# Second half of a linear-attention and MLP block: the attention product by seven products, the last two products by column block, the last stores on two queues

## The chip, the cores and the metric

The kernel runs on one core of one Trainium2 chip. The metric is the device time of one execution in microseconds, the median of the runs. The engines are TensorE (PE, with its weight loads listed as PEld), VectorE (DVE), ScalarE (ACT), GpSimd (POOL) and SyncE (SP, which here only issues DMAs).

## The reference

Input x is 2048 tokens of 512 features, all in float32. It is normalised, and two blocks are added to it: a linear attention with 32 heads and a two-layer MLP with a squared relu.

```python
xn = layernorm(x)
# A: q, k, v = xn @ wqkv, by head (H = 32, Dh = 16); phi(t) = (t + 1 if t > 0 else exp(t)) + 1e-6
kv = einsum("bhsd,bhse->bhde", phi(k), v)
z = phi(k) summed over s
o = (phi(q) @ kv) / (phi(q) . z + 1e-6)
A = o.reshape(B, S, D) @ wo
# B: F = 1376
r = max(xn @ w1 + b1, 0)
B = (r * r) @ w2 + b2
out = x + A + B
```

## The kernel before

**Precision.** Every float32 operand of a product is split into a high part and a rest (`split`: a copy on ACT into the reduced type, then a subtraction on DVE), and a product is three matmuls: high by high, rest by high, high by rest. Splits of weights ("ops") are written once to scratch in DRAM (`wd1`, `wd2`, `wdz`) and loaded back when needed; splits of activations ("s") are made just ahead of use by `parts_of` into one of five rotating tiles (`pair`).

**Stages.** The first stage takes the 16 tiles of 128 tokens one by one: normalise, transpose, keys, and the sum of phi(k) by x. From that sum the kernel forms kv and then `M = kv @ wo` per head, in four blocks of 128 rows which are written to DRAM (`wdm`). From there on the attention output is one product with `M`, whose rows stand beside those of `w2`. The second stage runs twice (`for n in range(2)`), each time over two blocks of 512 tokens, t1 and t2.

**One pass of the second stage.** A loop over `p` makes the hidden rows in pairs of 128-row tiles: `NQ = 2` pairs of queries (k = 0, 1) and `NP = 5` pairs of the MLP (k = 2 to 6), `NK = 7` in all. A pair of two tiles by two token blocks is a 2x2 block product, and `product` does it by seven block products instead of eight, with sums of weights made by `make_1` and sums of tokens `T[1]` to `T[4]`. The four results of pair k are `h[k, 0]` to `h[k, 3]` (relu and square for the MLP, phi and division for the queries).

The results are then multiplied by the rows of `w2` and `M`. In the first pass (n = 0) that is done directly, eight block products for each pair. In the second pass (n = 1) the MLP pairs go by seven products as well: `combinations(k)` makes sums of the four tiles on DVE, `make_t` made the matching sums of `w2` during the first pass (on DVE and ACT into the tiles `made`, which lie in the places `rp0` and `rp1`, and from there by a DMA to `wd2`). The tiles `rp0` and `rp1` are used again by the hidden tiles of the last pair (k = 6) of the second pass. Products 0 and 1 of an MLP pair are done inside the loop (`add_product`), products 4, 5, 3, 6, 7 behind it, in phases of one product over all five pairs (`phase_jobs`), which share two banks of PSUM named X, Y, Z, W and V. The attention pairs are done directly in this pass, by two groups of `attentions` (four tiles each, both halves of the columns), and each group ends with the odd eleventh row tile of the MLP (`z_job`, tile `hz`).

The order of jobs in the second pass is: Y by product 4, then attention and z on Z and Y, X by 5, Y by 3, X by 6, attention and z on V and W, V by 7. Between them, `copies` saves banks through ACT (`m1`, `m5`, `u2`), `add_to` adds on DVE, `turned_to` transposes on DVE and adds to the residual tile `res`, and `store` writes it out: eight DMAs of 128 KB for a block of 512 tokens, four for each half of the columns.

**Order.** All operations behind the first tiles are recorded and not issued at once. `Program.order` plays them through with estimated costs (`cost`) 60 times and issues them in the best order it found; PE's order is as recorded, that of the other engines is free within the dependencies. `nc.emit` issues all of them from one line, L295, so the profile tells them apart by tiles. A DMA is issued by SP, in its queue's order. Operands lie in eight places of 512 KB (`D0` to `D7`), filled in the order in which `needed_in` lists them as places come free.

`second` multiplies one pair of operand tiles by one split tile, six matmuls for two column blocks c, alternating between them; with `end` the last call does three for one block and then three for the other.

Of the kernel before, what the change touches and what calls it, by code (L numbers as in the profile page):

```python
# [12 lines left out]

P = 128
H = 32
REORDER = True


# [55 lines left out]
class Program:  # L74
# [60 lines left out]
    def cost(self, t, out, ins):  # L135
        n = 1
        for s, k in list(out.ap)[1:]:
            n *= k
        src = n
        for a in ins:  # L140
            m = 1
            for _, k in list(a.ap)[1:]:
                m *= k
            src = max(src, m)
        t.lock, t.size, t.lag = False, 0, 0.06
        if t.engine == "tensor":
            wide = t.name == "matmul" and ins[0].dtype != F32
            t.dur, t.lag = (0.0135 + n / 2400 if wide else 0.055 + n / 2400 if t.name == "transpose" else 0.11 + n / 1200), 0.23
        elif t.engine == "scalar":
            ps = any(map(in_psum, ins))  # L150
            t.dur = (0.2 if ps else 0.22) + src / 1250 + (0.09 if t.kw.get("bias") is not None and n > 64 and not isinstance(t.kw.get("bias"), float) else 0)
        elif t.engine == "vector":
            a, b = self.DVE.get(t.name, (0.1, 0.5))
            t.dur = a + src * b / 960
            t.lock = t.name in ("tensor_tensor", "scalar_tensor_tensor") and n > 64 and not any(map(in_psum, ins))
        elif t.engine == "gpsimd":
            t.dur = 0.2 + src * 2.3 / 1000 if t.name == "tensor_tensor" else 0.3
            t.lock = t.name == "tensor_tensor"
# [16 lines left out]
    def order(self):  # L175


        ts = self.tasks
        for t in ts:
            t.succs = []  # L180
        for t in ts:
            for place in t.first:
                for o in place.tasks:
                    t.preds.setdefault(o.index, 1)
            t.left = len(t.preds)
        for t in ts:
            for p, raw in t.preds.items():
                ts[p].succs.append((t, raw))
        line = [t for t in ts if not t.left]
        for t in line:  # L190
            for s, raw in t.succs:
                s.left -= 1
                if not s.left:
                    line.append(s)
        when = 0.0
        for t in ts:
            t.due = 1e9
            if t.engine == "tensor":
                t.due = when
                when += t.dur  # L200
        for t in reversed(line):
            e = t.engine
            took = t.dur if e != "sync" else t.lag + t.size / 320e3
# [29 lines left out]
    def play(self):  # L233
# [18 lines left out]
        while done < len(ts):  # L252
# [27 lines left out]
            if e == "sync":  # L280
                dma = end = max(dma, end) + t.size / 320e3
            done += 1
            for s, raw in t.succs:
                ready = end + (t.lag if e == "sync" or raw and s.engine != e else 0.0)
# [22 lines left out]
def kernel(  # L307
# [495 lines left out]
    def needed_in(n):  # L803
# [77 lines left out]

    ORDER = ((0, 0), (1, 0), (0, 1))

    def second(ps, key, s, first=False, last=False, end=False):

        a = op(*key)
        for n, (u, v), c in [(n, uv, c) for c in range(2) for n, uv in enumerate(ORDER)] if end else \
                [(n, uv, c) for n, uv in enumerate(ORDER) for c in range(2)]:
            nc.tensor.matmul(ps[c], lhsT=a[:, u * 256 + c * P:u * 256 + (c + 1) * P], rhs=s[:, v],
                             start=first and n == 0, stop=last and n == 2, skip_group_check=True)  # L890
        used()

    def second_z(ps, cs, s, first=False, last=False):
# [359 lines left out]
    for n in range(2):  # L1253
# [23 lines left out]
        def finish(k, i, src):  # L1277
# [9 lines left out]
            else:  # L1287
# [8 lines left out]
                elif n:  # L1296
                    square(o)

        def add_product(k, i):
            if n == 0:  # L1300
                for v in range(2):
                    second(acc[2 * v:2 * v + 2], ("2", k - NQ, 2 * i + v), s[k, i], k == NQ and i == 0)
            else:
                second(acc[2 * i:2 * i + 2], ("2", k - NQ, 2 * i), s[k, i], k == NQ)

        def combinations(k):

# [94 lines left out]
        if n == 0:  # L1402
# [14 lines left out]
            def step(e):  # L1417
# [6 lines left out]
                if e > 3:  # L1424
                    if not made_t and sorted(raw_free) == ["rp0", "rp1", "x0", "x1"]:
                        raw_free[:] = ["x0", "x1"]
                        raw_jobs.extend(raw_2(k, "t") for k in range(NP))
                        fetch_raws()
                    if len(raw_free) < 4:
                        for u in range(2 * (len(made_t) < NP)):  # L1430
# [21 lines left out]
            assert len(made_t) >= NP, made_t  # L1452
            do(outs, len(outs))
            do(columns, len(columns))
            do(sums, len(sums))
# [21 lines left out]
        def turned_to(t, a, src):  # L1477
            for c in range(2):
                add_turned(res[t], a + c, src[c])

        def strassen(ps, k, i, first=False, last=False):
            return lambda: h[k][i], lambda s: second(ps, ("2", k - NQ, i), s, first, last, i == 7 and last)

        def phase_jobs(ps, i, first=False, last=False):
            return [strassen(ps, k, i, first and k == NQ, last and k == NK - 1) for k in pairs_f]

        def attentions(ps, e, first, last):
            return [(lambda j=j: h[j // 2, e + j % 2], attention_job(ps, e, j, first and j == 0)[1]) for j in range(NJ)] +                    [(lambda: hz[:, e // 2], z_job(ps, e, last)[1])]
# [8 lines left out]
        o = {}  # L1497
        at_end(lambda: o.update(m5=copies("m5", Y)))
        jobs += attentions([*Z, *Y], 0, False, False)
        at_end(lambda: (add_to(m1, Z), turned_to(t1, 0, m1)))  # L1500
        jobs += phase_jobs(X, 5)
        at_end(lambda: o.update(u2=copies("u2", X)))
        jobs += phase_jobs(Y, 3, False, True)
        at_end(lambda: (add_to(o["u2"], Y), turned_to(t1, 2, o["u2"]), store(res[t1], t1, 0, 1)))
        jobs += phase_jobs(X, 6, False, True)
        at_end(lambda: (add_to(o["m5"], X), turned_to(t2, 0, X)))
        jobs += attentions([*V, *W], 2, True, False)
        at_end(lambda: (add_to(o["m5"], W), turned_to(t2, 2, o["m5"]), store(res[t2], t2, 1)))
        jobs += phase_jobs(V, 7, False, True)
        at_end(lambda: (turned_to(t2, 0, V), store(res[t2], t2, 0)))  # L1510

        def prepare_s(job):
            return parts_of("s", job[0]()) if job[0] else None
# [32 lines left out]
```

## Time and profile before

| | |
|---|---|
| time, median of 3 runs | 415.73 us (415.72 to 415.8) |
| profiled execution | 415.67 us, span 414.0 us |
| PE busy | 404.5 us, 1808 instructions |
| DVE busy | 326.8 us |
| ACT busy | 256.4 us |
| POOL busy | 27.8 us |
| DMA | 96.19 MB, mean 232 GB/s |
| granted PE clock | 0.998 |

Span is the time from the first to the last event of the profiled execution; the execution's own time also holds what lies around it. Busy time counts each engine's instructions by themselves; a share of the span says little about a single stage. The chain of waits follows the last instruction back to what released it. A timeline row gives start, length, engine, operation, tiles (out<-in), the count and, in brackets, how long the engine was idle before it and who ended that.

### The profile page before, as it was taken

To read this page: it belongs to the slowest core of one execution; us is meant where nothing else is said; L and a number is where in the kernel's file an instruction comes from. 1 tells how busy PE (TensorE), PEld (TensorE's weight loads), DVE (VectorE), ACT (ScalarE), POOL (GpSimd) and SP (SyncE) were. 2 spreads that over 40 slices of the span, in tenths; PEclk is the share of its full clock that TensorE was granted. 3 is DMA by queue.
4 is the path that set the end of the run, shared out by engine and by line. 5 is a ranking of instruction groups with operands and counts; after the bars stand their busy time and mean duration, and the time that the engine had idled before them with its cause. 6 is when DMAs were issued, how large, how long until landed. Compare 5 with 4: busy or idle time off the path is not lost.

```text
span 414.0 us, 5503 instructions
## 1 busy us (share of the span) xinstructions
PE 404.5 (98%) x1808; PEld 334.2 (81%) x1808; DVE 326.8 (79%) x551; ACT 256.4 (62%) x438; POOL 27.8 (7%) x48
## 2 busy tenths in 40 slices
PE   8999999999999999999999999999999999999993
PEld 7788888888888888888888888888888887888882
DVE  6898998899788989999989350999999766376943
ACT  5786665666777998899943220477877677335310
POOL 2242322220000000000000000000000000000000
PEclk9999999999999999999999999999999999999999
DMA  7862636914979786963999997897866589958604
GB/s 239 283 185 76 160 114 149 290 53 156 359 245 364 225 290 243 329 225 156 357 320 269 357 375 297 236 289 276 275 220 192 194 236 260 287 178 252 181 0 102
DMA packets 78272, 96.19 MB, mean 232 GB/s; under 512 B 40002, under 2 KB 51266, under 8 KB 77988
## 3 DMA queue, kind: packets, MB, share of 16 engines
q1 hardware_dynamic: 78244, 95.84, 74.1%
q8 instruction: 14, 0.23, 0.2%
q14 instruction: 14, 0.11, 0.1%
HBM read 59.91 MB, written 33.82 MB: 226 GB/s over the span
## 4 chain that ended last, share of the span: by engine, by line
PE 96%; DVE 2%; DMA 1%; ACT 0%; issue 0%
PE ps L295 51%; PE acc L295 45%; DMA x<-in_A_x_dram 1%; DVE res L295 0%; DVE o L295 0%; DVE st L295 0%; DVE xp L295 0%; DVE y L295 0%; ACT rr L295 0%; DVE mv L295 0%
## 5 line engine op out<-in xcount | busy, mean ns | idle before, releaser
L295 PE MATMUL ps<-s,ops 128*128 128x512 f32 x390 | 92.9, 389 | 0.0
L295 PEld LDWEIGHTS ps<-s,ops 128*128 128x128 f32 x390 | 73.1, 188 | 15.3 <-ACT s L295 0.2
L295 PE MATMUL acc<-s,ops 128*128 128x512 f32 x300 | 72.7, 390 | 0.8 <-ACT rr L295 0.8
L295 PEld LDWEIGHTS acc<-s,ops 128*128 128x128 f32 x300 | 56.2, 188 | 13.1 <-ACT rr L295 1.2
L295 PE MATMUL acc<-pk,tok 128*128 128x512 f32 x192 | 47.0, 394 | 0.0
L295 DVE TENSOR_TENSOR s<-rr,s 128x512 fp32r<-128x512 f32 x46 | 31.6, 689 | 17.2 <-ACT s L295 16.2
L295 ACT ACTIVATE s<-rr 128x512 fp32r<-128x512 f32 x46 | 28.9, 631 | 24.4 <-PE acc L295 13.9
L295 PEld LDWEIGHTS acc<-pk,tok 128*128 128x128 f32 x192 | 35.5, 188 | 7.8 <-DVE pk L295 0.5
L295 PE MATMUL ps<-T,ops 128*128 128x512 f32 x168 | 41.4, 390 | 0.0
L295 PE MATMUL acc<-T,ops 128*128 128x512 f32 x168 | 41.2, 389 | 0.0
L295 PEld LDWEIGHTS acc<-T,ops 128*128 128x128 f32 x168 | 31.5, 188 | 6.6
L295 PEld LDWEIGHTS ps<-T,ops 128*128 128x128 f32 x168 | 31.5, 188 | 6.5
L295 POOL TENSOR_TENSOR tok<-xp,tok 128x512 fp32r<-128x512 f32 x16 | 22.9, 1432 | 42.1 <-ACT tok L295 35.1
L295 PE MATMUL ps<-xs0h,ops 128*128 128x512 f32 x72 | 23.6, 389 | 0.0
L295 ACT ACTIVATE rr<-acc 128x512 f32<-128x512 f32 x23 | 13.5, 588 | 15.0 <-PE acc L295 14.8
L295 DVE TENSOR_TENSOR ops<-raw,ops 128x512 fp32r<-128x512 f32 (+1 forms) x28 | 18.7, 676 | 1.5 <-ACT ops L295 1.3
L295 ACT ACTIVATE k<-ps 128x512 f32<-128x512 f32 x16 | 9.5, 595 | 15.7 <-PE ps L295 15.6
L295 ACT ACTIVATE ops<-raw 128x512 fp32r<-128x512 f32 (+1 forms) x28 | 16.3, 593 | 4.4 <-PE acc L295 2.4
L295 PE MATMUL acc<-xs0h,ops 128*128 128x512 f32 x56 | 18.4, 389 | 0.0
L295 ACT ACTIVATE s<-rf 128x512 fp32r<-128x512 f32 x10 | 6.3, 633 | 18.0 <-PE ps L295 17.6
L295 DVE TENSOR_TENSOR rr<-acc,rr 128x512 f32<-128x512 f32 x21 | 14.4, 684 | 3.8 <-PE acc L295 1.7
L295 ACT ACTIVATE rr<-rr,odds 128x512 f32<-128x512 f32 x15 | 10.8, 723 | 9.2 <-DVE rr L295 9.1
(152 smaller groups left out, 734.5 us busy)
## 6 DMA issues: line engine op xcount, KB each, us to landing
ops<-wd SPq DMA_DIRECT2D x43, 512.0 KB, 5.3
wd<-ops SPq DMA_DIRECT2D x35, 512.0 KB, 4.8
ops<-wd SPq DMA_DIRECT2D x42, 256.0 KB, 3.8
wd<-made SPq DMA_DIRECT2D x10, 512.0 KB, 5.7
res<-in_A_x_dram SPq DMA_DIRECT2D x32, 128.0 KB, 6.0
out_dram<-res SPq DMA_DIRECT2D x32, 128.0 KB, 3.7
x<-in_A_x_dram SPq DMA_DIRECT2D x5, 512.0 KB, 6.3
raw<-in_B_w_dram SPq DMA_DIRECT2D x10, 256.0 KB, 5.2
```

The lines of the kernel that those rows point to most:

```text
L295: getattr(getattr(self.nc, t.engine), t.name)(*map(real, t.args), **{k: real(a) for k, a in t.kw.items()})
```

## The change

In the second pass the attention pairs join the seven products. `make_t` now also makes combined weights for the two pairs of `M`, `combinations` is also run for k = 0 and 1, and the products 0 and 1 of these pairs become four direct jobs at the front of the job list, into the banks X and Z that `add_product` uses. The phases run over seven pairs, in the order 2, 3, 4, 5, 0, 1, 6. The groups `attentions` are gone; `second_z` stands alone where they were. The first phase comes after the direct jobs.

In the last phase (product 7 into V) the last two pairs, 1 and 6, are held back and done together: all six matmuls of column block 0, then all six of column block 1. Of the last four stores two are issued by ACT instead of SP. The planner's cost function is taught that ACT can issue a DMA.

```diff
+LAST = 2
...
-        elif t.engine == "scalar":
+        elif t.engine == "scalar" and t.name != "dma_start":
...
-        keys = [("2", f, 4) for f in range(NP)]
-        keys.insert(NP - 2, ("2", NP - 1, 2))
+        keys = [("2", f, i) for f in (NP, NP + 1) for i in (0, 2)]
+        keys.insert(3, ("2", NP - 1, 2))
...
+        order = (*range(NP - 1), NP, NP + 1, NP - 1)
+        keys += [("2", f, 4) for f in order]
         flush_keys()
-        attention(False)
         both_of("z", 0, 2)
-        keys += [("2", f, i) for i in (5, 3, 6) for f in range(NP)]
+        keys += [("2", f, i) for i in (5, 3, 6) for f in order]
         flush_keys()
-        attention(False)
         both_of("z", 0, 2)
-        keys += [("2", f, 7) for f in range(NP)]
+        keys += [("2", f, 7) for f in order]
...
-    def second(ps, key, s, first=False, last=False, end=False):
-
-        a = op(*key)
-        for n, (u, v), c in [(n, uv, c) for c in range(2) for n, uv in enumerate(ORDER)] if end else \
-                [(n, uv, c) for n, uv in enumerate(ORDER) for c in range(2)]:
+    def second(ps, key, s, first=False, last=False, before=None):
+
+        todo = [(op(*k), b) for k, b in (before or []) + [(key, s)]]
+        steps = [(n, uv, c, k) for n, uv in enumerate(ORDER) for c in range(2) for k in range(1)]
+        if before:
+            steps = [(n, uv, c, k) for c in range(2) for k in range(len(todo)) for n, uv in enumerate(ORDER)]
...
-    def store(r, t, *halves):
+    def store(r, t, *halves, by=None):
         for g, h, rows in out_blocks(of, t):
             if h in halves:
-                nc.sync.dma_start(rows, r[g, h])
+                (by or nc.sync if g.start % 64 else nc.sync).dma_start(rows, r[g, h])
...
-                        raw_jobs.extend(raw_2(k, "t") for k in range(NP))
+                        raw_jobs.extend(raw_2(k, "t") for k in range(NK))
...
-        pairs_f = range(NQ, NK)
+        pairs_f = (*range(NQ, NK - 1), *range(NQ), NK - 1)
...
+        def combined(k, i):
+            if k not in h:
+                run(*combinations(k))
+            return h[k][i]
...
-        m1 = copies("m1", X)
-        jobs, ends = phase_jobs(Y, 5 - 1, True), {}
...
-        jobs.insert(NP - 2, (None, lambda s: add_product(NK - 1, 1)))
+        jobs = [direct(k, i) for k in range(NQ) for i in range(2)]
+        ends[4] = [lambda: o.update(m1=copies("m1", X))]
+        jobs += phase_jobs(Y, 4, True)
+        jobs.insert(3, (None, lambda s: add_product(NK - 1, 1)))
         at_end(lambda: o.update(m5=copies("m5", Y)))
-        jobs += attentions([*Z, *Y], 0, False, False)
+        jobs.append((lambda: hz[:, 0], lambda s: second_z([*Z, *Y], range(NJ), s)))
...
-        jobs += attentions([*V, *W], 2, True, False)
+        jobs.append((lambda: hz[:, 1], lambda s: second_z([*V, *W], range(NJ), s, True)))
...
         jobs += phase_jobs(V, 7, False, True)
-        at_end(lambda: (turned_to(t2, 0, V), store(res[t2], t2, 0)))
+        at_end(lambda: (turned_to(t2, 0, V), store(res[t2], t2, 0, by=nc.scalar)))
```

More of the change, by code (lines that the diff above doesn't have):

```diff
@@ L202, in order @@
             e = t.engine
-            took = t.dur if e != "sync" else t.lag + t.size / 320e3
+            took = t.dur if not t.size else t.lag + t.size / 320e3
             for s, raw in t.succs:
@@ L279, in play @@
             last = max(last, end)
-            if e == "sync":
+            if t.size:
                 dma = end = max(dma, end) + t.size / 320e3
@@ L283, in play @@
             for s, raw in t.succs:
-                ready = end + (t.lag if e == "sync" or raw and s.engine != e else 0.0)
+                ready = end + (t.lag if t.size or raw and s.engine != e else 0.0)
                 if ready >= s.ready:
@@ L882 @@
     ORDER = ((0, 0), (1, 0), (0, 1))
-    def second(ps, key, s, first=False, last=False, end=False):
-        a = op(*key)
-        for n, (u, v), c in [(n, uv, c) for c in range(2) for n, uv in enumerate(ORDER)] if end else \
-                [(n, uv, c) for n, uv in enumerate(ORDER) for c in range(2)]:
-            nc.tensor.matmul(ps[c], lhsT=a[:, u * 256 + c * P:u * 256 + (c + 1) * P], rhs=s[:, v],
-                             start=first and n == 0, stop=last and n == 2, skip_group_check=True)
+    def second(ps, key, s, first=False, last=False, before=None):
[3 more added lines that the diff above has]
+            steps = [(n, uv, c, k) for c in range(2) for k in range(len(todo)) for n, uv in enumerate(ORDER)]
+        for n, (u, v), c, k in steps:
+            a, b = todo[k]
+            nc.tensor.matmul(ps[c], lhsT=a[:, u * 256 + c * P:u * 256 + (c + 1) * P], rhs=b[:, v],
+                             start=first and n == 0 and k == 0, stop=last and n == 2 and k == len(todo) - 1, skip_group_check=True)
         used()
@@ L1297, in finish, with row_of @@
                     square(o)
+        def row_of(k):
+            return k - NQ if k >= NQ else NP + k
         def add_product(k, i):
@@ L1303, in add_product @@
             else:
-                second(acc[2 * i:2 * i + 2], ("2", k - NQ, 2 * i), s[k, i], k == NQ)
+                second(acc[2 * i:2 * i + 2], ("2", row_of(k), 2 * i), s[k, i], k == NQ)
         def combinations(k):
@@ L1426, in step @@
                         raw_free[:] = ["x0", "x1"]
-                        raw_jobs.extend(raw_2(k, "t") for k in range(NP))
+                        raw_jobs.extend(raw_2(k, "t") for k in range(NK))
                         fetch_raws()
                     if len(raw_free) < 4:
-                        for u in range(2 * (len(made_t) < NP)):
+                        for u in range(2 * (len(made_t) < NK)):
                             make_t(len(made_t), u)(work.tile([P, 2, 512], F32R, name="made", tag=f"rp{u}"))
@@ L1451 @@
                      lambda j: prepare(j), 2, step)
-            assert len(made_t) >= NP, made_t
+            assert len(made_t) >= NK, made_t
             do(outs, len(outs))
@@ L1479, in turned_to, with direct @@
                 add_turned(res[t], a + c, src[c])
+        def combined(k, i):
+            if k not in h:
+                run(*combinations(k))
+            return h[k][i]
         def strassen(ps, k, i, first=False, last=False):
-            return lambda: h[k][i], lambda s: second(ps, ("2", k - NQ, i), s, first, last, i == 7 and last)
+            return lambda: combined(k, i), lambda s: later.append((("2", row_of(k), i), s)) if i == 7 and k in pairs_f[-LAST:-1] else                     second(ps, ("2", row_of(k), i), s, first, last, later if i == 7 and last else None)
         def phase_jobs(ps, i, first=False, last=False):
-            return [strassen(ps, k, i, first and k == NQ, last and k == NK - 1) for k in pairs_f]
-        def attentions(ps, e, first, last):
-            return [(lambda j=j: h[j // 2, e + j % 2], attention_job(ps, e, j, first and j == 0)[1]) for j in range(NJ)] +                    [(lambda: hz[:, e // 2], z_job(ps, e, last)[1])]
-        m1 = copies("m1", X)
-        jobs, ends = phase_jobs(Y, 5 - 1, True), {}
+            return [strassen(ps, k, i, first and k == pairs_f[0], last and k == pairs_f[-1]) for k in pairs_f]
+        def direct(k, i):
+            return lambda: h[k, i], lambda s: second(acc[2 * i:2 * i + 2], ("2", row_of(k), 2 * i), s, False, i == 0 and k == NQ - 1)
+        o, ends, later = {}, {}, []
         def at_end(f):
             ends.setdefault(len(jobs) - 1, []).append(f)
-        jobs.insert(NP - 2, (None, lambda s: add_product(NK - 1, 1)))
-        o = {}
+        jobs = [direct(k, i) for k in range(NQ) for i in range(2)]
+        ends[4] = [lambda: o.update(m1=copies("m1", X))]
+        jobs += phase_jobs(Y, 4, True)
+        jobs.insert(3, (None, lambda s: add_product(NK - 1, 1)))
         at_end(lambda: o.update(m5=copies("m5", Y)))
-        jobs += attentions([*Z, *Y], 0, False, False)
-        at_end(lambda: (add_to(m1, Z), turned_to(t1, 0, m1)))
+        jobs.append((lambda: hz[:, 0], lambda s: second_z([*Z, *Y], range(NJ), s)))
+        at_end(lambda: (add_to(o["m1"], Z), turned_to(t1, 0, o["m1"])))
         jobs += phase_jobs(X, 5)
```

## The prediction

> **What bounds the kernel.** I read the page's busy times first, then its chain of waits, then busy time by stretch of the span, then the timeline of the stretches that the change touches. All lines are L295, the one place where recorded operations are issued, so tiles tell the operations apart.
>
> ```profile
> PE 404.5 (98%) x1808; PEld 334.2 (81%) x1808; DVE 326.8 (79%) x551; ACT 256.4 (62%) x438; POOL 27.8 (7%) x48
> PE 96%; DVE 2%; DMA 1%; ACT 0%; issue 0%
> 268.00:300.00 32.00, 32.00 (x142) 26.43 (x141) 29.43 (x50) 24.83 (x41) 0.00 (x0) 1.00 0.86 280
> 300.00:345.00 45.00, 44.22 (x195) 36.15 (x194) 35.93 (x58) 33.48 (x56) 0.00 (x0) 1.00 0.74 213
> 345.00:366.00 21.00, 21.00 (x94) 17.37 (x93) 8.68 (x13) 8.58 (x15) 0.00 (x0) 1.00 1.04 275
> ```
>
> TensorE (PE) carries the span: 98% busy, 96% of the chain. The three stretches (start:end, length, then busy time of PE, PEld, DVE, ACT, POOL, the granted clock 1.00, DMA share, GB/s) say where that could end: VectorE (DVE) has 2.57 us free in 268 to 300 and 9.07 in 300 to 345, ScalarE (ACT) 7.2 and 11.5. After 345 both are half idle. So a matmul removed is worth its whole spacing, and work added to DVE or ACT costs nothing while it fits and keeps out of the way of a copy for which PE waits.
>
> **Part 1: twelve matmuls fewer.** In the second half of the kernel the attention product was 8 jobs of two `second` calls, 16 x 6 = 96 matmuls; now it is 2 pairs x 7 products x 6 = 84. The built order of instructions has 1771 rows on PE instead of 1783, and the first 1506 are the same. The price of one is its spacing in an undisturbed stretch:
>
> ```profile
> 218.09 40.80 PE ps L295 x180
> ```
>
> 40.80 / 180 = 0.2267 us, so 12 x 0.2267 = **-2.72**. The Trainium skill (TensorE: Matmul & The Clock Gate, Back-to-back issue gap) gives about 131 ns sustained for N=512 and 216 ns isolated; by those the term would be an estimated -1.6 or -2.6. The trace disagrees with the first and decides.
>
> **Part 2: a stall that goes.** Between the two halves of this stage PE stands still once:
>
> ```profile
> 341.80 1.52 PE L295 MATMUL acc<-T,ops 128*128 128x512 f32 x6
> 343.36 0.69 ACT L295 ACTIVATE rr<-acc,odds 128x512 f32<-128x512 f32 x1
> 344.10 4.42 PE L295 MATMUL acc<-s,ops 128*128 128x512 f32 x18 [0.78 <-ACT rr L295]
> 348.35 1.52 PE L295 MATMUL ps<-s,ops 128*128 128x512 f32 x6
> ```
>
> Six matmuls from 341.80 end at 343.16; 18 more would end at 347.24, but the next group starts at 348.35: 1.11 us lost, because the first seven-product phase goes into the bank that ACT is just emptying (the relu at 343.36). Now 30 direct matmuls (four attention jobs and the moved `add_product`) stand first, in banks that already accumulate, and the phase starts 6.8 us later: **-1.11**. What is next late there: the direct jobs need splits of attention tiles that DVE finished with long before; the `add_product` is now the fourth group, at 343.16 + 18 x 0.2267 = 347.24, and its input follows the same relu. In the new order two more splits of 0.63 stand between ACT's steps there, so the split is ready near 346; I count no wait. Bounds for this part: -0.4 to -1.11.
>
> **Part 3: work added beside it.** Combined weights for two more pairs (four `make_t`), combinations of two attention pairs, and splits for 14 jobs instead of 8:
>
> ```profile
> L295 DVE TENSOR_TENSOR t<-raw_t 128x256 f32<-128x256 f32 x10 | 4.2, 421 | 0.1
> L295 DVE TENSOR_TENSOR made<-t,made 128x512 fp32r<-128x512 f32 x10 | 6.7, 680 | 0.0
> L295 DVE TENSOR_TENSOR rr<-rr 128x512 f32<-128x512 f32 x9 | 6.1, 682 | 0.5 <-ACT rr L295 0.3
> L295 DVE TENSOR_TENSOR s<-rr,s 128x512 fp32r<-128x512 f32 x46 | 31.6, 689 | 17.2 <-ACT s L295 16.2
> L295 ACT ACTIVATE made<-t 128x512 fp32r<-128x512 f32 x10 | 6.6, 658 | 4.5 <-DMA wd<-made 3.4 <-DVE t L295 1.1
> L295 ACT ACTIVATE s<-rr 128x512 fp32r<-128x512 f32 x46 | 28.9, 631 | 24.4 <-PE acc L295 13.9 <-DVE s L295 10.2
> 345.40 0.69 DVE L295 TENSOR_TENSOR s<-rr,s 128x512 fp32r<-128x512 f32 x1 [0.78 <-ACT s L295]
> ```
>
> DVE gains 4 x (2 x 0.42 + 0.68) = 6.1, 8 x 0.68 = 5.5 and 6 x 0.69 = 4.1, in all 15.7 us; ACT 4 x 0.66 + 6 x 0.63 = 6.4. Up to the split of the last pair's second tile (345.40) the new order puts on DVE all 6.1 of the weights, 5 of the 8 combinations (3.4), and four splits pulled in against five operations pushed out (-0.7): 8.8 us, into 2.57 + 9.07 = 11.6 free. It fits, with little to spare. The rest falls into the half idle stretch after 345. SP gets four more loads and four more stores for the weights and loads single operands (256 KB) where it loaded four pairs of them twice; with a DMA share of 0.74 to 0.86 in these stretches I count nothing for it, and rival (c) prices the case where that cover is gone.
>
> One place does not fit. ACT's order changes near 276:
>
> ```profile
> 269.87 0.71 DVE L295 STREAM_TRANSPOSE db<-da 128x512 f32<-128x512 f32 x1 [0.72 <-ACT da L295]
> 275.42 0.63 DVE L295 TENSOR_TENSOR rr<-acc,rr 128x512 f32<-128x512 f32 x1
> 276.61 0.60 ACT L295 ACTIVATE rr<-acc 128x512 f32<-128x512 f32 x1 [1.04 <-PE acc L295]
> 279.70 0.58 ACT L295 ACTIVATE rr<-acc 128x512 f32<-128x512 f32 x1
> 280.18 0.71 ACT L295 ACTIVATE e<-rr,odds 128x512 f32<-128x512 f32 x1
> 280.49 1.52 PE L295 MATMUL acc<-T,ops 128*128 128x512 f32 x6
> ```
>
> PE's group at 280.49 needs the copy that ends at 279.70 + 0.58 = 280.28 and starts 0.21 behind it: no slack. The exponential `e` (0.71), which stood behind that copy, now stands ahead of the copy at 276.61, and waits for the DVE add at 275.42. Ahead of that add DVE now has one `made` and two `t` (about 1.35 with their overlap) where it idled 0.72, so the add ends near 276.05 + 0.63 = 276.7, `e` near 277.45, and the copies behind it, which follow each other without a gap, come 0.85 late. Behind the waiting `e` stand all of ACT's copies, and PE behind them: **+0.85**, between 0 and 1.5. Everything later moves by as much, which relaxes the other close places of the loop.
>
> **Part 4: a new wait for the copies of `m5`.** Behind the first phase PE goes on into Z and then Y, while ACT copies Y:
>
> ```profile
> 352.40 1.09 ACT L295 ACTIVATE m<-acc 128x512 f32<-128x512 f32 x2 [0.50 <-PE acc L295]
> 352.43 1.52 PE L295 MATMUL ps<-s,ops 128*128 128x512 f32 x6
> 353.79 1.52 PE L295 MATMUL acc<-s,ops 128*128 128x512 f32 x6
> ```
>
> Before, six matmuls into Z (1.36) covered the 1.09 of the copies. Now `second_z` follows directly: two matmuls into Z (0.45), then Y. The second copy ends 1.06 after the phase, the matmul into that bank was due after 0.68, and a released matmul starts about 0.2 later (as at 280.28 above): **+0.6**, from 0.2 to 1.1.
>
> **Part 5: the tail.**
>
> ```profile
> 400.03 6.96 PE L295 MATMUL ps<-s,ops 128*128 128x512 f32 x30
> 406.35 0.72 DVE L295 STREAM_TRANSPOSE o<-ps 128x512 f32<-128x512 f32 x1 [1.91 <-PE ps L295]
> 408.45 0.69 DVE L295 TENSOR_TENSOR res<-o,res 128x512 f32<-128x512 f32 x1
> 409.17 0.85 SPq L295 DMA_DIRECT2D out_dram<-res  x2
> 410.62 0.52 SPq L295 DMA_DIRECT2D out_dram<-res  x1
> 410.00:411.00 1.00, 0.00 (x0) 0.00 (x0) 0.00 (x0) 0.00 (x0) 0.00 (x0) 1.00 0.88 189
> 411.00:412.00 1.00, 0.00 (x0) 0.00 (x0) 0.00 (x0) 0.00 (x0) 0.00 (x0) 1.00 0.98 201
> ```
>
> PE ends at 400.03 + 30 x 0.2267 = 406.83, DVE 2.31 later, at 409.14. The first column block was complete three matmuls before the end; now, with the last two products taken block by block, six (1.36) before. Its transpose and add (1.4) are then done when the second block is ready, and DVE ends near 0.2 + 0.74 + 0.69 = 1.63 behind PE: **-0.7**, at least 0. The last four stores go out from 409.17 to 410.62, one after the other on SP; with two on ACT, which is idle, the last would go out about 1.1 earlier. The Trainium skill (DMA: Bandwidth & Descriptors, Issuing engines are not separate DMA queues) says that this saves only issue time, usually small beside the transfer. The rows bear that out in part: the engines' share is 0.88 and 0.98 while the stores run. I take half of the 1.1: **-0.5**, from 0 to -1.1.
>
> **Sum.** The profiled execution took 415.67 (span 414.0), the median of the runs is 415.73. 415.67 - 2.72 - 1.11 + 0.85 + 0.6 - 0.7 - 0.5 = **412.1**.
>
> **Rivals.** (a) *Two queues give nothing*: the 16 engines are the limit, as the share of 0.98 suggests, and the skill's page named in part 5 says so. Then 412.6. Against it: 0.88 in the first microsecond leaves room. (b) *DVE is too full*: of the 11.6 us free only half is usable because its gaps are waits for ACT and PE; then the last pair's split is some 3 us late and PE waits 2 to 3.5 us: 414 to 415.6, faster or no change. For it: 29.43 busy of 32. Against it: the order lets combinations that nobody awaits slide behind. (c) *Slower: the last pair's tiles wait for a DMA.* The two tiles `rp0`, `rp1` now serve seven pairs of combined weights, and the loop's last pair writes into them at once after:
>
> ```profile
> wd<-made SPq DMA_DIRECT2D x10, 512.0 KB, 5.7
> 323.19 0.69 DVE L295 SCALAR_TENSOR_TENSOR rr<-rr,dr 128x512 f32<-128x512 f32 x1
> 329.76 0.60 ACT L295 ACTIVATE rr<-acc 128x512 f32<-128x512 f32 x1
> 332.53 0.58 ACT L295 ACTIVATE rr<-acc 128x512 f32<-128x512 f32 x1
> 327.00 5.44 PE acc L295 x24
> ```
>
> The copies at 329.76 and 332.53 must wait until the stores of the last two `made` tiles have landed; they stand in ACT's queue ahead of all its later copies, so PE would follow. The second `made` stands in DVE's new order right behind the operation of 323.19; done by 324.5, stored on SP in order behind an operand load, landed 5.7 later, at 330.2: 3.2 us in hand with the shift of part 3. Each microsecond beyond that is one on PE; the gain of 3.6 is gone when the store lands 6.8 late, and at 8 late the time is 416.9. Behind those stores on SP stand operand loads; the load for the first direct group (343.16) waits for the matmuls that end as the group at 327.00 begins, 16 us ahead of its use, so the tiles decide and not the loads. (d) That the change does not do what it says: the built order shows 84 matmuls, so only the waits can differ.
>
> **Chances.** Forecast 0.67; (a) 0.15; (b) 0.11, of which 0.05 faster, 0.05 no change and 0.01 slower; (c) 0.07, of which 0.06 slower and 0.01 no change. A measurement of this kernel can tell 0.2% (0.8 us) from no change. Faster 0.87, same 0.06, slower 0.07. Range: the bounds of the stalls and of the tail, moved together in part, give 410.4 below; above it takes in (a) and the lower part of (b): 414.3. What is left out is (c), the rest of (b), and some 0.05 below.
>
> **What would show it.** In the changed profile: PE with 12 matmuls fewer and no wait before the first direct group near 344; a wait of PE for `rr` on ACT near 280; a wait for `m` of about half a microsecond where `second_z` begins; DVE ending 1.6 us behind PE; last stores issued within 0.5 us. Wrong would be: PE waits of over 1 us in 285 to 345 (b), ACT waiting for `wd<-made` near 333 (c), or the last bytes landing no sooner behind DVE's end (a).

## The result and the profile after

| | before | after |
|---|---|---|
| median | 415.76 us (6 runs, 415.64 to 416.06) | 412.01 us (6 runs, 411.87 to 412.64) |
| ratio | | 0.9912, 95% interval 0.9899 to 0.9924 |
| profiled execution | 415.67 us, span 413.96 us | 411.98 us, span 410.28 us |

A second set of runs of the changed kernel, beside other runs of the kernel before, gave 412.18 us (0.9913, 0.9900 to 0.9927). The forecast was 412.1.

All recorded operations now lie on L296. The page of the changed kernel (busy times, chain), then its busy time by stretch, in the stretches that the prediction used:

```profile
PE 402.3 (98%) x1796; PEld 332.1 (81%) x1796; DVE 340.5 (83%) x577; ACT 261.6 (64%) x448; POOL 27.9 (7%) x48
PE 96%; DVE 2%; DMA 1%; issue 0%
268.00:300.00 32.00, 32.00 (x143) 26.32 (x142) 29.98 (x54) 25.11 (x41) 0.00 (x0) 1.00 0.89 294
300.00:345.00 45.00, 45.00 (x200) 37.28 (x199) 41.57 (x69) 34.14 (x57) 0.00 (x0) 1.00 0.88 261
345.00:366.00 21.00, 20.99 (x92) 16.83 (x91) 15.70 (x25) 11.64 (x21) 0.00 (x0) 1.00 1.02 277
```

TensorE still carries the span, with twelve matmuls fewer and no idle time in 300 to 345 (before: 44.22 of 45). VectorE took 13.7 us more in all, of which 5.64 lie in that stretch and 7.02 in the next; it is now busy for 41.57 of 45 there, and still nobody on TensorE waits for it.

The old stall's place, and the place of `second_z`, in the timeline of the changed kernel:

```profile
343.27 6.96 PE L296 MATMUL ps<-s,ops 128*128 128x512 f32 x30
350.07 9.68 PE L296 MATMUL acc<-s,ops 128*128 128x512 f32 x42
359.57 1.08 ACT L296 ACTIVATE m<-acc 128x512 f32<-128x512 f32 x2 [0.50 <-PE acc L296]
359.59 0.61 PE L296 MATMUL ps<-s,ops 128*128 128x512 f32 x2
360.22 0.99 PE L296 MATMUL acc<-s,ops 128*128 128x512 f32 x2
360.70 0.19 PEld L296 LDWEIGHTS acc<-s,ops 128*128 128x128 f32 x1 [0.30 <-ACT m L296]
```

30 direct matmuls start at 343.27 and the first phase follows at 350.07, exactly 30 x 0.2267 later: the stall of before is gone. Behind the phase, two matmuls into Z run while ScalarE copies Y, and then TensorE waits. By the spacing of the matmuls' starts (0.397, 0.488 and 0.341 us where 0.2267 is undisturbed) that costs 0.17, 0.26 and 0.11 us, 0.55 in all.

The tail, in the timeline and in stretches of one microsecond:

```profile
397.81 6.05 PE L296 MATMUL ps<-s,ops 128*128 128x512 f32 x26
402.54 0.72 DVE L296 STREAM_TRANSPOSE o<-ps 128x512 f32<-128x512 f32 x1 [0.66 <-PE ps L296]
404.65 0.69 DVE L296 TENSOR_TENSOR res<-o,res 128x512 f32<-128x512 f32 x1
405.37 0.85 SPq L296 DMA_DIRECT2D out_dram<-res  x2
405.37 0.93 ACTq L296 DMA_DIRECT2D out_dram<-res  x2
406.00:407.00 1.00, 0.00 (x0) 0.00 (x0) 0.00 (x0) 0.00 (x0) 0.00 (x0) 0.51 0.67 150
407.00:408.00 1.00, 0.00 (x0) 0.00 (x0) 0.00 (x0) 0.00 (x0) 0.00 (x0) 0.50 0.94 188
408.00:409.00 1.00, 0.00 (x0) 0.00 (x0) 0.00 (x0) 0.00 (x0) 0.00 (x0) 0.50 0.84 187
```

The last four stores now go out side by side, two on each queue, and the last issue ends at 406.30, 0.96 behind VectorE's end at 405.34; before it was 2.0 (411.14 behind 409.14). Yet the span ends 4.93 behind VectorE's end (410.276 and 405.342), and before it ended 4.81 behind it (413.958 and 409.146).

### The profile page after: what moved, and what is told of

It reads as the page before. It is cut to its first block, busy times and chain, and to the rows that moved or that the text cites. A ratio compares the mean times of both kernels' runs of the same rounds, so it can differ in the third digit from the quotient of the medians.

```text
span 410.3 us, 5553 instructions
## 1 busy us (share of the span) xinstructions
PE 402.3 (98%) x1796; PEld 332.1 (81%) x1796; DVE 340.5 (83%) x577; ACT 261.6 (64%) x448; POOL 27.9 (7%) x48
## 4 chain that ended last, share of the span: by engine, by line
PE 96%; DVE 2%; DMA 1%; issue 0%
PE ps L296 52%; PE acc L296 44%; DMA x<-in_A_x_dram 1%; DVE res L296 0%; DVE o L296 0%; DVE st L296 0%; DVE xp L296 0%; DVE y L296 0%; DVE mv L296 0%
## 5 line engine op out<-in xcount | busy, mean ns | idle before, releaser
L296 PE MATMUL ps<-s,ops 128*128 128x512 f32 x402 | 94.2, 389 | 0.0
L296 PEld LDWEIGHTS ps<-s,ops 128*128 128x128 f32 x402 | 75.5, 188 | 15.7
L296 PE MATMUL acc<-s,ops 128*128 128x512 f32 x276 | 66.0, 390 | 0.0
L296 PEld LDWEIGHTS acc<-s,ops 128*128 128x128 f32 x276 | 51.7, 188 | 11.7 <-ACT m L296 0.7
L296 PE MATMUL acc<-pk,tok 128*128 128x512 f32 x192 | 47.1, 394 | 0.0
L296 ACT ACTIVATE s<-rr 128x512 fp32r<-128x512 f32 x50 | 31.4, 631 | 21.4 <-DVE s L296 13.1
L296 DVE TENSOR_TENSOR s<-rr,s 128x512 fp32r<-128x512 f32 x50 | 34.2, 688 | 11.2 <-ACT s L296 10.2
L296 PEld LDWEIGHTS acc<-pk,tok 128*128 128x128 f32 x192 | 35.5, 188 | 7.8 <-DVE pk L296 0.6
L296 PE MATMUL ps<-T,ops 128*128 128x512 f32 x168 | 41.4, 390 | 0.0
L296 PE MATMUL acc<-T,ops 128*128 128x512 f32 x168 | 41.3, 390 | 0.0
L296 PEld LDWEIGHTS acc<-T,ops 128*128 128x128 f32 x168 | 31.5, 188 | 6.7 <-ACT rr L296 0.2
L296 PEld LDWEIGHTS ps<-T,ops 128*128 128x128 f32 x168 | 31.5, 188 | 6.5
L296 POOL TENSOR_TENSOR tok<-xp,tok 128x512 fp32r<-128x512 f32 x16 | 23.0, 1440 | 41.6 <-ACT tok L296 38.2
L296 PE MATMUL ps<-xs0h,ops 128*128 128x512 f32 x72 | 23.6, 389 | 0.0
L296 ACT ACTIVATE rr<-acc 128x512 f32<-128x512 f32 x23 | 13.5, 587 | 15.9 <-PE acc L296 15.9
L296 DVE TENSOR_TENSOR ops<-raw,ops 128x512 fp32r<-128x512 f32 (+1 forms) x28 | 18.6, 675 | 1.6 <-ACT ops L296 1.3
L296 ACT ACTIVATE k<-ps 128x512 f32<-128x512 f32 x16 | 9.5, 592 | 15.4 <-PE ps L296 15.3
L296 ACT ACTIVATE ops<-raw 128x512 fp32r<-128x512 f32 (+1 forms) x28 | 16.3, 593 | 4.4 <-PE acc L296 2.4
L296 ACT ACTIVATE s<-rf 128x512 fp32r<-128x512 f32 x10 | 6.3, 633 | 19.2 <-PE ps L296 18.2
L296 PE MATMUL acc<-xs0h,ops 128*128 128x512 f32 x56 | 18.4, 389 | 0.0
L296 DVE TENSOR_TENSOR rr<-acc,rr 128x512 f32<-128x512 f32 x21 | 14.5, 688 | 2.6 <-PE acc L296 1.4
L296 PEld LDWEIGHTS ps<-xs0h,ops 128*128 128x128 f32 x72 | 13.5, 188 | 2.8
```

The costliest lines, as they stand in the source:

```text
L296: getattr(getattr(self.nc, t.engine), t.name)(*map(real, t.args), **{k: real(a) for k, a in t.kw.items()})
```

## Experiments

The numbers of one kernel's time in these sections are medians; in brackets stands the ratio to the kernel before with its 95% interval. Each kernel is the changed kernel with one edit, unless it is said otherwise.

### What twelve matmuls are worth

```diff
-        keys += [("2", f, i) for i in (5, 3, 6) for f in order]
+        keys += [("2", f, i) for i in (5, 3, 6) for f in order if i != 6 or f < NP]
-        jobs += phase_jobs(X, 6, False, True)
+        jobs += [j for k, j in zip(pairs_f, phase_jobs(X, 6, False, True)) if k >= NQ]
```

> The changed kernel with twelve matmuls left out: the sixth-index product of the two attention pairs (their loads and splits too), so that part of the result is missing. Theory (TensorE is the bound through the whole of the second stage, and one matmul is worth its spacing of 0.2267 us): 2.72 us faster, 409.3. Rival (something else, VectorE at 17.45 us of 24 or the loads, is close behind and takes over): 410.5 or more. By the 131 ns that the Trainium skill gives for a sustained matmul (TensorE: Matmul & The Clock Gate, Back-to-back issue gap) an estimate would be 410.4.

Measured: 410.29, ratio to the kernel before 0.9868 (0.9852 to 0.9883), 1.72 faster than the changed kernel and not 2.72. Yet from the first wait near 360 to the last matmul's start the trace is 2.72 us shorter: 360.05 to 400.58, where it was 360.22 to 403.47. The missing microsecond is at the end: VectorE ends 2.9 earlier, but the span ends 6.04 behind it and not 4.93. SP's waits from 390 on, and the engines' share in two stretches:

```profile
SPq L296 <- DMA out_dram<-res: 2.6, 1, 2.6
405.00:406.00 1.00, 0.00 (x0) 0.00 (x0) 0.00 (x0) 0.00 (x0) 0.00 (x0) 0.50 0.37 83
406.00:407.00 1.00, 0.00 (x0) 0.00 (x0) 0.00 (x0) 0.00 (x0) 0.00 (x0) 0.50 0.59 130
```

SP stood 2.6 us in front of its last store until an earlier store had landed, and the last store ran alone. The built program says which: transfers are given eight landing semaphores (the counters that a landed transfer raises) in turn, and each waits until the last transfer with its semaphore has landed. The turn is dealt out in an order in which ACT's two stores stand ahead of stores that SP issues sooner; with two transfers fewer, SP's last store came eight places behind ACT's first, and had to wait for it: ACT's, issued at 402.48, landed at 405.38, and SP's was issued at 405.40. In the changed kernel the turn happens to fall so that no store waits. So the theory was tested again with all last stores on SP:

> The same twelve matmuls left out as in the kernel before (the sixth-index product of the two attention pairs, so that part of the result is missing), and all four last stores on SP. Theory (TensorE gave back 2.72 us there; 1.1 us of it were lost because the last store on SP waited 2.6 us for an earlier store to land, which the one queue avoids): 412.05 - 2.72 = 409.3. Rival (the last stores come too close behind the four before them, whichever queue issues them): 410.3.

Measured: 409.37 (0.9845, 0.9831 to 0.9858), 2.72 below the one-queue kernel's 412.09 further down. TensorE is the bound through this part of the kernel, and a matmul is worth 0.2267 us there.

### The place of the first phase

```diff
-        jobs = [direct(k, i) for k in range(NQ) for i in range(2)]
-        ends[4] = [lambda: o.update(m1=copies("m1", X))]
-        jobs += phase_jobs(Y, 4, True)
+        jobs = phase_jobs(Y, 4, True)
         jobs.insert(3, (None, lambda s: add_product(NK - 1, 1)))
         at_end(lambda: o.update(m5=copies("m5", Y)))
+        jobs += [direct(k, i) for i in range(2) for k in range(NQ)]
+        ends[len(jobs) - 3] = [lambda: o.update(m1=copies("m1", X))]
```

The list of operands is put in the same order. The direct products now read tiles that `combinations` has already overwritten, so this part of the result is another one.

> The changed kernel with the old place of the first seven-product phase: product 4 of all pairs goes into Y right behind the loop, as before the change, and the direct products of the two attention pairs follow it. The planner works out the order of the other engines anew. Theory (the 1.1 us stall at 344 came from the phase going into the bank that ScalarE was still emptying, so it comes back; and 24 direct matmuls now stand between the phase and second_z, so the 0.55 us of waits for the copies of m5 go): 412.0 + 1.1 - 0.55 = 412.55. Rival (the stall was the order of the old splits and not the place of the phase): only the 0.55 goes, 411.5.

Measured: 413.02 (0.9935, 0.9922 to 0.9947). TensorE's one wait in 330 to 365, and the group behind it:

```profile
PEld acc L296 <- ACT rr L296: 1.2, 1, 1.2
344.44 4.42 PE L296 MATMUL acc<-s,ops 128*128 128x512 f32 x18 [0.78 <-ACT rr L296]
```

It is the old stall in the old place with the old releaser, and no wait for `m` is left. By the starts of the matmuls it costs 0.94 + 0.11 = 1.05 us, and the 0.55 near 360 are gone. The time is 0.5 above the theory. Of that, 0.23 is there when the stall begins: the last matmul ahead of it starts at 343.28, in the changed kernel at 343.05. The trace puts it down to the order of the other engines, which was worked out anew: from 10 to 55 us the two traces agree within 0.07, then TensorE waits at 56.41 for VectorE's `pk`, where the changed kernel does not wait, and is 0.49 late, part of which is made up later. Another 0.22 lies behind VectorE's end (5.15 to the end of the span, not 4.93). The rival (411.5) is out.

### How much room VectorE has

```diff
                     s[k, i] = parts_of(f"s{n}_{k}_{i}", o)
+                    if n:
+                        nc.twice.append(nc.tasks[-1])
...
-            getattr(getattr(self.nc, t.engine), t.name)(*map(real, t.args), ...)
+            for _ in range(1 + (t in self.twice)):
+                getattr(getattr(self.nc, t.engine), t.name)(*map(real, t.args), ...)
```

> The changed kernel in which VectorE makes ten of its splits twice, the second time writing the same values: the lower parts of the first two tiles of each MLP pair in the second loop, 10 x 0.68 = 6.8 us more on VectorE between 288 and 348; the order of every engine is otherwise the same. This measures how near the prediction's rival (b) was. Theory (VectorE had 3.43 us free in 300 to 345 and about 1 just before, and is in order, so about 2.5 us of the 6.8 find no room and TensorE waits as long): 413.5 to 415, with TensorE gaps between 320 and 348. Rival (the work slides into the half idle stretch behind 345 and TensorE never waits): 412.0.

Measured: 415.96, 1.0002 of the kernel before (0.9993 to 1.0011): the whole gain is gone, and more than the theory allowed. Its busy times in 300 to 345, the waits of TensorE's loads there, and the last of them:

```profile
300.00:345.00 45.00, 42.71 (x185) 34.08 (x184) 42.90 (x72) 31.70 (x53) 0.00 (x0) 1.00 0.83 244
PEld ps L298 <- DVE s L298: 4.0, 4, 1.2
342.24 0.73 PE L298 MATMUL ps<-s,ops 128*128 128x512 f32 x2 [0.66 <-DVE s L298]
```

VectorE is not full (42.90 of 45), but TensorE waits once in each pass of the loop (303, 316, 329 and 342), 1.0, 1.0, 0.4 and 0.9 us by the spacing of its starts, for the split that the product inside the loop takes: 3.4 of the 3.95 us. Two doubled splits put up to 1.4 us ahead of that product, and about 1.0 of it shows. The trace of the changed kernel has the difference: there that split ends 0.44, 0.36, 0.46 and 0.46 us before the weight load that takes it (301.80, 314.04, 326.28 and 338.52). In the third pass VectorE stood idle for 0.45 just ahead of the split, which took up some more. So the room is not the sum of VectorE's gaps, as rival (b) of the prediction and this theory both counted it: it is what that one split has in hand, some 0.4 us in each pass.

### The cover for the copies of `m5`

```diff
+        z = sorted(self.two_banks, key=lambda t: t.start)
+        for t, start in zip([t for k in range(2) for t in z if (z.index(t) % 4) // 2 == k], [t.start for t in z]):
+            t.start = start
```

`two_banks` holds the twelve matmuls of the first `second_z`; their places in TensorE's order are dealt out anew, Z first.

> The changed kernel with the twelve matmuls of the first second_z in another order: the six into Z first, then the six into Y, where they alternated two by two; nothing else moves on any engine. Theory (TensorE waits 0.17, 0.26 and 0.11 us there, 0.55 in all, for ScalarE's two copies out of Y, and six matmuls of 0.227 us cover them): 0.55 us faster, 411.45, with no start gap over 0.26 us near 360. Rival (TensorE is only let go earlier into the next wait, for the banks or splits of the next phase): 412.0.

Measured: 411.67 (0.9903, 0.9889 to 0.9916). The timeline near 360:

```profile
359.60 1.09 ACT L300 ACTIVATE m<-acc 128x512 f32<-128x512 f32 x2 [0.50 <-PE acc L300]
359.63 1.52 PE L300 MATMUL ps<-s,ops 128*128 128x512 f32 x6
360.99 1.52 PE L300 MATMUL acc<-s,ops 128*128 128x512 f32 x6
```

The six matmuls into Z cover the copies and TensorE does not wait. Its last start comes at 402.92 and not at 403.47, 0.55 sooner. The median is 0.34 to 0.51 below the two of the changed kernel.

### The tail: column blocks

The last two products one after the other again, only the last by blocks:

```diff
-LAST = 2
+LAST = 1
-        if before:
+        if before is not None:
```

> The changed kernel with one thing undone: the last two products are no longer taken column block by column block; only the last one is, so that the first block is complete three matmuls before the end and not six. Theory (VectorE's transposes and adds set the tail: it ends 1.64 us behind the last matmul now, 2.31 us before): 0.67 us slower, 412.7. Rival (the tail's stores are bound elsewhere, so that 0.67 us of VectorE do not show): 412.0.

Measured: 413.16 (0.9934, 0.9921 to 0.9946), slower by 1.15 and not by 0.67. VectorE ends 2.54 behind TensorE's last start (406.34 and 403.80), where it was 1.87 (405.34 and 403.47): 0.67, as expected. The rest is 0.32 by which this execution was late already at 281, and 0.2 behind VectorE's end. Most of the 0.32 is there at the first product of the keys (8.13, where it was 7.83), long before anything that the edit touches; whether the other four executions (412.76 to 413.19) began late too, no trace says. Because of that difference the same edit was put alone into the kernel before:

> The kernel before with one part of the change done alone: the last two products taken column block by column block; no product is added or removed, the stores stay on SP, no other engine's order moves. Theory (VectorE then ends 0.67 us earlier behind TensorE, as in the changed kernel, and the tail behind VectorE is as long as it was): 415.8 - 0.67 = 415.1. Rival (undoing this part in the changed kernel cost 1.15 us and that was its true worth): 414.65.

Measured: 415.28, 0.9988 (0.9979 to 0.9997), that is 0.55 faster. VectorE ends 1.87 behind the last start (408.63 and 406.76). So the part is worth 0.67 in the traces; the medians give 0.55 and 1.15 on its two sides.

> The changed kernel once more, on the same chip and beside the same runs of the kernel before, as a measure for the others. Theory: 412.0. Rival (the profiled executions differ by up to 0.55 us in how late their first 281 us are, and so may the chips): up to 412.6.

Measured: 412.18, as told above; the rival's 412.6 was no median's.

### The tail: two queues

```diff
-        at_end(lambda: (turned_to(t2, 0, V), store(res[t2], t2, 0, by=nc.scalar)))
+        at_end(lambda: (turned_to(t2, 0, V), store(res[t2], t2, 0)))
```

> The changed kernel with one thing undone: all four last stores are issued by SP again, none by ACT. Theory (the DMA engines set the end of the tail, not the issuing queue: from the first packet on, their share is 0.87 to 1.09 in half microseconds for about 2.5 us both before and after, and DVE's end to the span's end took 4.82 us with one queue and 4.96 with two): no change, 412.0, within 0.2 us. Rival (issue on one queue costs the 0.5 us that the prediction gave it): 412.5.

Measured: 412.09 (0.9911, 0.9898 to 0.9925), between the two medians of the changed kernel. From the first packet of the last four stores to the last one took 2.81 us; with two queues it took 2.70 and 2.94 in the two traces of the changed kernel, and 2.77 in the kernel before. The second queue is worth nothing here. Whether issue can be a limit at all was tried with smaller stores: the last column block is turned, added and stored in two halves of its rows, so that the first half's stores leave sooner, together with Z first.

```diff
+        def finale():
+            add_turned(res[t2], 0, V[0])
+            o = w512("o", "d", 2)[:, :256]
+            for e in range(2):
+                add_turned_part(res[t2], 1, V[1], e, o)
+                store_part(res[t2], t2, 0, e, nc.scalar)
+        at_end(finale)
```

> The changed kernel with second_z as in the kernel with Z first, and with the last column block turned, added and stored in two halves of its rows, each half's four stores of 64 KB on the two queues. Theory (the tail behind TensorE is one transpose, one add, 0.87 us to the first packet, 2.6 us in which the 16 DMA engines are full, and 1.4 us behind; halves let the first packets go 0.7 us sooner and the engines stay full): 411.67 - 0.7 = 411.0. Rival (four issues of 0.45 us on each queue, or a wait for the landing of an earlier store, leave the engines idle between): 411.7.

Measured: 412.85 (0.9928, 0.9914 to 0.9942), slower by 1.2 than Z first alone. SP's waits from 400 on, and the stretch behind the first half:

```profile
SPq L300 <- DMA out_dram<-res: 3.1, 1, 3.1
405.00:406.00 1.00, 0.00 (x0) 0.00 (x0) 0.47 (x2) 0.00 (x0) 0.00 (x0) 1.00 0.31 66
```

The turn of the eight semaphores again: in the built program the last of the four stores before these waits for ACT's first to land (at 406.36), all of SP's later stores stand behind it, and in the microsecond shown the engines are two thirds idle. In the next kernel those four stores alternate between the queues too, which moves the turn:

```diff
-        at_end(lambda: (add_to(o["m5"], W), turned_to(t2, 2, o["m5"]), store(res[t2], t2, 1)))
+        at_end(lambda: (add_to(o["m5"], W), turned_to(t2, 2, o["m5"]), store(res[t2], t2, 1, by=nc.scalar)))
```

> The kernel with Z first and the last column block in two halves, with one more thing changed: the four stores before the last eight (the other half of the columns of the same tokens) alternate between SP and ACT as well, so that on the list of landing semaphores, which every eighth transfer shares, no store of SP stands eight behind a store of ACT that is issued later. Theory (the 1.2 us by which the halves were slower came from SP's 3.1 us wait for a landing; without it the engines are full from the first half's first packet on, which comes 0.5 us sooner than without halves): 411.67 - 0.5 = 411.15, and SP waits for no landing for over 0.5 us. Rival (eight stores of 64 KB cost their issue and fixed times more often than the earlier start is worth): 411.7 to 412.5.

> The kernel with Z first and the last column block in two halves, all stores on SP. Theory (eight issues of 0.45 us now end 3.6 us behind the first half's add, where the engines would need 2.6 us for the same bytes: here the issuing queue is the limit, which it was not with four stores of twice the size): 0.7 us slower than Z first alone, 412.4, with DMA shares of about 0.7 while the last stores run. Rival (issue is no limit here either, and the earlier start counts): 411.15.

Measured: 411.28 with both queues (0.9892, 0.9876 to 0.9909), 412.21 with all stores on SP (0.9910, 0.9895 to 0.9924). Two stretches of the last stores, of the first kernel and then of the second:

```profile
405.00:406.00 1.00, 0.00 (x0) 0.00 (x0) 0.12 (x1) 0.00 (x0) 0.00 (x0) 1.00 0.89 186
406.00:407.00 1.00, 0.00 (x0) 0.00 (x0) 0.00 (x0) 0.00 (x0) 0.00 (x0) 0.88 0.85 180
```

```profile
406.00:407.00 1.00, 0.00 (x0) 0.00 (x0) 0.00 (x0) 0.00 (x0) 0.00 (x0) 1.00 0.62 132
407.00:408.00 1.00, 0.00 (x0) 0.00 (x0) 0.00 (x0) 0.00 (x0) 0.00 (x0) 1.00 0.59 128
```

With 64 KB a store and one queue the engines' share is flat at 0.6, a store in half a microsecond (64 KB at 132 GB/s): here the issuing queue is the limit, and the second one is worth 0.93. One wait of SP for a landing is left in the faster kernel, 1.1 us and not the 0.5 at most that was expected. At 411.28 it is the lowest median of the kernels here that leave no product out; what it gains over Z first (0.39) is less than the spread of single runs of either, so the order of these two is likely and not sure.

## Why the prediction was right

| step | forecast | in the trace |
|---|---|---|
| twelve matmuls fewer | -2.72 | -2.72 |
| stall behind the loop | -1.11 | -1.05 |
| `e` ahead of ScalarE's copies | +0.85 | +0.09 |
| copies of `m5` | +0.6 | +0.55 |
| column blocks | -0.7 | -0.67 |
| two queues | -0.5 | +0.12 |
| not counted: a wait of 0.07 at 301 gone, 0.11 late before 281 | | +0.04 |
| sum | -3.6 | -3.6 |

The sum agrees with the span, which is 3.68 shorter (413.96 to 410.28). What is left lies in the matmuls right behind a wait, which start up to 0.013 us further apart than 0.2267; with them the stall is worth 1.11 and the copies of `m5` cost 0.58. Four steps held to 0.06 us. Two did not, by 0.76 and 0.62, and in opposite directions: that the total fits is in part luck.

**Part 1** held, by the trace and by the twelve matmuls taken out in another place. The 131 ns of the Trainium skill (TensorE: Matmul & The Clock Gate, Back-to-back issue gap) are not reached in this stage; twelve matmuls moved the time by 2.72 us and not by an estimated 1.57.

**Part 2** held at its upper end: 1.05 by the starts of the two matmuls that wait, 1.11 with those behind them. The place of the phase was the cause, since putting it back brings the wait back.

**Part 3** was mis-sized in one step. The added work fitted, as forecast: VectorE took on 26 instructions, as counted, for 13.7 us of busy time; the forecast of 15.7 added their single times, which overlap. But `e` was to wait for a VectorE add that one `made` and two `t` would delay. First what VectorE did some ten microseconds earlier in the kernel before (the first and the last of four `t`), then the steps of VectorE, ScalarE and TensorE in the changed kernel:

```profile
266.41 0.41 DVE L295 TENSOR_TENSOR t<-raw_t 128x256 f32<-128x256 f32 x1
267.54 0.42 DVE L295 TENSOR_TENSOR t<-raw_t,t 128x256 f32<-128x256 f32 x1
```

```profile
268.00 0.68 DVE L296 TENSOR_TENSOR made<-t,made 128x512 fp32r<-128x512 f32 x1
269.18 0.43 DVE L296 TENSOR_TENSOR t<-raw_t,t 128x256 f32<-128x256 f32 x1
275.43 0.69 DVE L296 TENSOR_TENSOR rr<-acc,rr 128x512 f32<-128x512 f32 x1 [0.29 <-PE acc L296]
276.15 0.72 ACT L296 ACTIVATE e<-rr,odds 128x512 f32<-128x512 f32 x1 [1.50 <-DVE rr L296]
279.95 0.58 ACT L296 ACTIVATE rr<-acc 128x512 f32<-128x512 f32 x1
280.60 1.64 PE L296 MATMUL acc<-T,ops 128*128 128x512 f32 x6
```

The add starts at 275.43, in the profile before at 275.42, and it even waits 0.29 for TensorE ahead of it. The prediction added what the new order put in front of the add, and did not take off what the same order had taken away there: the four `t` that stood at 266.41 to 267.96, about as long as the `made` and two `t` that came (268.00 to 269.61). So `e` ran 0.55 sooner than forecast (276.15 and not 276.7), in ScalarE's idle time, and the copy that TensorE needs moved by 0.25 (279.70 to 279.95), 0.11 of which this execution was late anyway. This is read from the two traces; no run put the four `t` back.

**Part 4** held (0.55), and Z first shows that the missing cover was the cause. The 0.2 that it added for the release was about right: TensorE's held load starts 0.05 behind the copy (360.70 and 360.65), and the matmul behind it comes 0.11 late.

**Part 5**: the column blocks held. The two queues did shorten the issue (the last one ends 1.04 sooner behind VectorE, though the four take 0.93 and not the 0.5 named as a sign) and gave nothing: rival (a) is true for this term. The engines are at 0.94 and 0.84 while the four stores run, as they were at 0.88 and 0.98 before, and need 2.7 to 2.9 us for the half megabyte whoever issues it; half of the issue time was no estimate to take. The 0.12 in the table is no cost of the second queue either: from VectorE's end to the end of the span took 4.93 and 5.14 in the two traces with two queues and 4.96 in the one with one. The Trainium skill (DMA: Bandwidth & Descriptors, Issuing engines are not separate DMA queues) says that starting DMAs from several engines saves only the time of starting them, usually small beside the transfer. The runs agree with it: 412.09 with one queue, 412.01 and 412.18 with two. With stores of half the size the issue time that it calls usually small was the limit, and worth 0.93.

**Rival (b)** did not come, but it was nearer than its chance of 0.11 says: 6.8 us more on VectorE cost 3.95. The check to make was the slack of each split (0.36 to 0.46 us) and not the free time of a stretch.

**Rival (c)** did not come: the last store of a `made` tile was issued at 320.97. Its landing is not in the trace; the last two before it whose landing is took 4.9 and 5.4 us. The copies that write those places start at 329.87 and 333.98, and ScalarE's waits in 320 to 340 name no DMA:

```profile
ACT rr L296 <- DVE rr L296: 4.4, 5, 1.0
ACT rr L296 <- PE acc L296: 1.1, 2, 0.9
```

## What to carry to other kernels

Work out a wait from the new order as a whole, with what left the queue as well as what joined it; and ask of an engine beside the bound not how much time it has free but how much the one operation has in hand that the bound takes next. In these runs a second queue paid only where the engines were not full while the stores ran, which one line of the transfer share tells. Before moving transfers between queues, look at which of them share a landing semaphore.

## What the runs showed of the hardware

Executions of the same instructions differ: the matmul group that the changed kernel starts at 280.60 sees its one wait end at 280.92 there, and between 280.71 and 281.26 in the profiles of the other kernels that share that code. That is 0.55 us, most of which is there at the first product of the keys (7.68 to 8.13), and it is as much as the smaller steps here are worth. So those are read from the distances inside a trace and not from the medians.

On VectorE halves cost more than half: a transpose of 256 columns took 0.45 us and one of 512 took 0.72, an add 0.43 and 0.69.
